# DMA transposes in the first DFT step of batches 2 to 7 and in half of batch 0's turn

## The chip, the cores and the metric

The kernel runs on one core of one Trainium2 chip. The number that counts is device time in microseconds (us), the median of several runs. Beside it stands one profiled execution, from which all durations below come. A core has TensorE (PE; its weight loads are listed as PEld), VectorE (DVE), ScalarE (ACT), GpSimd (POOL) and SyncE (SP); each works through its own instructions in order, and semaphores tie them together. DMAs are issued by SP (plain and transposing) and by POOL (those that cast from f32 to f16), and 16 DMA engines carry them out.

## The reference, cut to what matters

```python
def _attn_ref(x, w_r, w_i, b_r, b_i):            # x: 8 x 3008 x 256
    X = np.fft.rfft(x, axis=1)
    Xr, Xi = X.real, X.imag
    Yr = Xr @ w_r - Xi @ w_i + b_r
    Yi = Xr @ w_i + Xi @ w_r + b_i
    Yr = np.sign(Yr) * np.maximum(np.abs(Yr) - 0.01, 0.0)
    Yi = np.sign(Yi) * np.maximum(np.abs(Yi) - 0.01, 0.0)
    return np.fft.irfft(Yr + 1j * Yi, n=x.shape[1], axis=1)

def _moe_ref(x, w_in, w_out, s, b):              # x: 24064 x 256, d_ff 2048
    r = np.maximum(x @ w_in, 0.0)
    return (s * (r * r) + b) @ w_out
```

The output of the first function, seen as 24064 rows, is the input of the second. Inputs and output are float32.

## The kernel before, in words

The length 3008 is 94 x 32, so each transform is done in two DFT steps, both as matmuls with f16 tables: one over n1 (94 points, giving 96 rows that the code calls kappa), one over n2 (32 points). Kappa rows come in groups of four, so a pair table works on 128 rows (4 kappa x 32 n2), 24 pairs in all (NPAIR; H is 12).

For one batch the steps are:

- **s1** (`s1_units`): first DFT step over n1. 16 units; each multiplies x16 (f16 copy of x, 94 rows) by A_t, which is the stationary operand, with 512 columns of x moving. The result u (96 rows) goes to DRAM (ud, four stores of 384 KB) and comes back (us, four loads of 384 KB) with (kappa, n2) on the partitions.
- **s23** (`s23_units`): second forward step with F_t, channel mixing with W_t and W_g, soft threshold, rows put together in `ring` by small SP DMAs, first inverse step with T_t, result v. v goes to DRAM (vd, six stores) and comes back as vs (two loads of 768 KB) with kappa on the partitions.
- **s4** (`s4_units`): last inverse step with C_t, result yt, transposed for the feed-forward part.

Then come the tiles of the feed-forward part: `first_mm` (w_in, then Relu on ACT and square on DVE or ACT) and `second_mms` (w_out, then scale and bias on DVE, then the store). A tile has 16 values of mc; one value is a slot. The dictionary `plan` says which units of s1, s23 and s4 of later batches are put into which slot, and `schedule(start, span, units)` spreads them evenly. `mark[b]` is the slot of batch b's first tile; a period from one mark to the next has 96 slots, or 80 for batch 2. While the tiles of batch b-2 run, s1 of batch b and s23 of batch b-1 run in the same period, and s4 of batch b-1 ends just before mark[b-1]. `evac` moves a PSUM result to SBUF on ACT or DVE, whichever has less in the running sum `load`. Pools limit what may be alive at once: us has five buffers of a quarter batch, vs two halves, u three chunks, the output buffers ost three.

Batch 0 (`first_batch`) is handled alone, since nothing runs beside it yet. Its own first step writes ut with channels on the partitions, the mixing is done before the second forward step (`mix`, `fwd_dft`, `inv_dft`, 12 steps of i), and the result vt (channel half ec on partitions) is turned by TensorE with an identity: `turn(ec, k)`, eight matmuls and an evacuation of 1024 columns into vs, for k in 0 to 3 and both ec. `last_dft` then does the last step. While this goes on, the compact tables F_c and T_c are loaded and copied into zeroed block tables: `place_f(0)` and `place_f(1)` on ACT, `place_f_2` and `place_t` on DVE. A few units of batch 1's s1 run at the end (`some`), six are left for the first slots of the main loop (`schedule(0, 10, more)`). POOL loads x of batch 1, w_in and w_out after a gate on T_c, then makes W_g, the bounds, and w_sum (a sum over w_out); `make_bias` in slot 15 multiplies w_sum by ones on TensorE (L336).

The order within each engine is not exactly that of the source: the tile layer that records the program places the instructions. Each DMA also waits for the DMA eight places earlier on its queue, whose semaphore it takes over.

Of the kernel before, what the change touches and what calls it, by code (L numbers as in the profile page):

```python
# [9 lines left out]
F16 = mybir.dt.float16  # L10
F32 = mybir.dt.float32
# [3 lines left out]
P = 128  # L15
# [81 lines left out]
def kernel(  # L97
# [26 lines left out]
    F_d = nc.inline_tensor(fwd.astype(np.float16), name="dft_fwd").ap()  # L124
    T_d = nc.inline_tensor(inv.astype(np.float16), name="dft_inv").ap()
# [14 lines left out]
    upool = ctx.enter_context(tc.tile_pool(name="up", bufs=3))  # L140
    uspool = ctx.enter_context(tc.tile_pool(name="usp", bufs=5))
# [3 lines left out]
    vspool = ctx.enter_context(tc.tile_pool(name="vsp", bufs=2))  # L145
# [70 lines left out]
    b_g = cpool.tile([P, 2, D], F32, name="b_g")  # L216
# [4 lines left out]
    F_c = uspool.tile([P, NPAIR, 2, N2], F16, name="F_c", tag="us")  # L221
    b_h = cpool.tile([P, D], F16, name="b_h")
# [4 lines left out]
    sel_t = cpool.tile([P, P], F16, name="sel_t")  # L227
    T_c = uspool.tile([P, NPAIR, 64], F16, name="T_c", tag="us")
# [9 lines left out]

    def emit_load_forward():
        nc.sync.dma_start(  # L240
            out=F_c[:, 0:H].rearrange("p q r k -> p q (r k)"), in_=F_d[:, 0:H]
        )
        nc.sync.dma_start(out=sel_t, in_=S_d)

    def emit_load_inverse():
        nc.sync.dma_start(
            out=F_c[:, H:].rearrange("p q r k -> p q (r k)"), in_=F_d[:, H:]
        )
        t_load = nc.sync.dma_start(out=T_c, in_=T_d)
        with tc.issue_after(t_load.ins):  # L250
            nc.sync.dma_start(out=eye_t, in_=E_d)
            nc.sync.dma_start(out=C_t, in_=C_d)
            for i, bv in enumerate((b_r, b_i)):
                nc.sync.dma_start(out=b_st[:, i], in_=bv.unsqueeze(0).to_broadcast([P, D]))
            nc.sync.dma_start(out=s_bc, in_=moe_s.unsqueeze(0).to_broadcast([P, 1]))
            nc.sync.dma_start(out=bb_bc, in_=moe_b.unsqueeze(0).to_broadcast([P, 1]))
# [15 lines left out]
    F_t = cpool.tile([P, NPAIR, P], F16, name="F_t")  # L272
    nc.vector.memset(F_t, 0.0)
    T_t = cpool.tile([P, NPAIR, P], F16, name="T_t")
    nc.vector.memset(T_t, 0.0)
    F_2 = [uspool.tile([P, H, P], F16, name="F_2", tag="us") for _ in range(2)]
    for f in F_2:
        nc.gpsimd.memset(f, 0.0)
# [21 lines left out]
    def place_f(h):  # L300
        q = slice(h * H, h * H + H)
        for a in range(2):
            r = slice(64 * a, 64 * a + 64)
            nc.scalar.copy(out=blocks(F_t)[r, q, :, a], in_=F_c[r, q])

    def place_f_2(h):

        q = slice(h * H, h * H + H)
        for a in range(2):
            r = slice(64 * a, 64 * a + 64)  # L310
            nc.vector.tensor_scalar_mul(
                out=blocks(F_2[h])[r, :, 0, a], in0=F_c[r, q, 1], scalar1=-1.0
            )
            nc.vector.tensor_copy(out=blocks(F_2[h])[r, :, 1, a], in_=F_c[r, q, 0])

    def place_t(h):
        q = slice(h * H, h * H + H)
        for i in range(4):
            r = slice(32 * i, 32 * i + 32)
            c = 64 * (i % 2)  # L320
            nc.vector.tensor_copy(out=T_t[r, q, c : c + 64], in_=T_c[r, q])
# [12 lines left out]
    def make_bias():  # L334
        ps = other_bank()
        nc.tensor.matmul(ps[:, 0:D], ones, w_sum, start=True, stop=True)  # L336
        for j in range(2):
            nc.scalar.activation(
                out=bias_bc[:, j], in_=ps[:, 0:D], func=AF.Copy, scale=bb_bc
            )  # L340

# [8 lines left out]
    def first_batch():  # L350
# [3 lines left out]
        for g in range(N2 // 4):  # L354
# [26 lines left out]
            if c == 2:  # L381
                with tc.issue_after(last_dve.ins):
                    nc.vector.memset(F_c[0:1, H, 0, 0:1], 0.0)
                    nc.vector.memset(T_c[0:1, 0, 0:1], 0.0)
                emit_load_inverse()
# [3 lines left out]
        with tc.issue_after(last_dve.ins), tc.issue_after(last_act.ins):  # L389
            place_f(0)  # L390
            place_f_2(0)

        gate = nc.gpsimd.tensor_copy(out=w_in_t[0][0:1, 0:1], in_=T_c[0:1, 0, 0:1])
# [6 lines left out]
        vt = bigpool.tile([P, DC, N2, 96], F16, name="vt", tag="corr")  # L400
        gs = {}
        zt = {}
        g_last = [None]

        def mix(ec, u):
# [10 lines left out]
            if u % 3 == 1:  # L416
                g_last[0] = nc.scalar.copy(out=g, in_=ps)
                load["act"] += 1.02
            else:
                g_last[0] = nc.vector.tensor_tensor(  # L420
                    out=g, in0=ps,
                    in1=b_g[:, :, ec * P : (ec + 1) * P].unsqueeze(1).to_broadcast([P, 4, 2, P]),
                    op=ALU.add,
                )
                load["dve"] += 1.2
# [29 lines left out]
        def inv_dft(ec, u):  # L455
            ps = other_bank()
            z = zt.pop((ec, u))
            for j in range(4):
# [5 lines left out]
                vt[:, ec, :, 16 * u : 16 * u + 16],  # L464
# [3 lines left out]
        for h in range(2):  # L468
            vs[(0, h)] = vspool.tile([96, HW, D], F16, name="vs", tag="vs")

        def turn(ec, k):
            ps = two_banks()
            for j in range(8):
                nc.tensor.matmul(
                    ps[0:96, j // 4, (j % 4) * P : (j % 4) * P + P],
                    vt[:, ec, 8 * k + j, :], eye_t, start=True, stop=True,
                )
            h, n = divmod(8 * k, HW)
            evac(
                vs[(0, h)][:, n : n + 8, ec * P : (ec + 1) * P],  # L480
                ps[0:96].rearrange("p h (j e) -> p (h j) e", e=P), 1024,
            )
# [3 lines left out]
        def last_dft(ec, n2):  # L486

            ps = [one_bank(), other_bank()]
            for j in range(8):
                h, k = divmod(n2 + j, HW)  # L490
                nc.tensor.matmul(
                    ps[j // 4][:, (j % 4) * 96 : (j % 4) * 96 + 96],
                    vs[(0, h)][:, k, ec * P : (ec + 1) * P], C_t,
# [8 lines left out]
        more = s1_units(1, True)  # L502
# [7 lines left out]
        for i in range(2 * U + 2):  # L510
# [6 lines left out]
            k = i - U - 2  # L517
            if 0 <= k < 4:
                turn(0, k)
            if 0 <= k - 1 < 4:  # L520
                last_dft(0, 8 * (k - 1))
            if i >= 2 * U:
                some(3)
            if i == 0:
                with tc.issue_after(g_last[0].ins):
                    place_t(0)
            if i == 1:
                with tc.issue_after(g_last[0].ins):
                    place_f(1)
            if i == 2:  # L530
                with tc.issue_after(g_last[0].ins):
                    place_f_2(1)
            if i == 3:
                with tc.issue_after(g_last[0].ins):
                    place_t(1)
            if i == 9:

                gate = nc.gpsimd.tensor_copy(out=low[0:1, 0, 0:1], in_=vt[0:1, 1, 0, 0:1])
# [4 lines left out]
        for k in range(4):  # L543
            turn(1, k)
            some(1)
            if k:
                last_dft(1, 8 * (k - 1))
        last_dft(1, 24)
# [3 lines left out]
    def s1_units(b, more_banks=False):  # L552

        ud = dpool.tile([96, N2, D], F16, name="ud", tag="ud")
        hold = {}

        def unit(i):
            c, j = divmod(2 * i, XCH)
            if j == 0:
                hold["u"] = upool.tile([P, XCH, D], F16, name="u", tag="u")  # L560
            ps = other_bank() if more_banks and i % 2 else one_bank()
# [4 lines left out]
            u = hold["u"]  # L566
            evac(u[0:96, j : j + 2, :], ps[0:96, :].rearrange("p (j d) -> p j d", j=2), 512)
            if j == XCH - 2:
                nc.sync.dma_start(
                    out=ud[:, c * XCH : (c + 1) * XCH, :], in_=u[0:96]  # L570
                )
            if i == N2 // 2 - 1:
                uv = ud.rearrange("k n d -> (k n) d").rearrange("(q p) d -> p q d", p=P)
                for q in range(4):
                    t = uspool.tile([P, 6, D], F16, name="us", tag="us")
                    nc.sync.dma_start(out=t, in_=uv[:, 6 * q : 6 * q + 6, :])
                    us[(b, q)] = t

        return [lambda i=i: unit(i) for i in range(N2 // 2)]

    def s23_units(b):
# [8 lines left out]
        def fwd_unit(i):  # L590
# [3 lines left out]
            t = us[(b, i // 3)]  # L594
            for j in range(2):
                q = (2 * i + j) % 6
                for dc in range(DC):
                    nc.tensor.matmul(  # L598
                        ps[:, :, dc, j, :], t[:, q, dc * P : (dc + 1) * P],
# [53 lines left out]
        def inv_unit(i):  # L653
# [15 lines left out]
            if i == H - 1:  # L669
                vv = vd.rearrange("q (k n) e -> (q k) (n e)", n=N2)  # L670
                for h in range(2):
                    t = vspool.tile([96, HW, D], F16, name="vs", tag="vs")
                    nc.sync.dma_start(
                        out=t.rearrange("k n e -> k (n e)"),
                        in_=vv[:, h * HW * D : (h + 1) * HW * D],
                    )
                    vs[(b, h)] = t
# [17 lines left out]
    def s4_units(b):  # L695
# [6 lines left out]
        def unit(g):  # L702
# [5 lines left out]
            for j in range(w):  # L708
                h, k = divmod(n2 + j, HW)
                nc.tensor.matmul(  # L710
                    ps[:, j * 96 : (j + 1) * 96],
                    vs[(b, h)][:, k, ec * P : (ec + 1) * P], C_t,
# [148 lines left out]
    def load_x_2():  # L861
        emit_load_x(2, us[(1, 3)][0:1, 0, 0:1])
# [5 lines left out]
    schedule(0, 10, more)  # L868
# [4 lines left out]
    for b in range(2, B):  # L873
        s0, s1, s2 = mark[b - 2], mark[b - 1], mark[b]
        p = s1 - s0
        schedule(s0 + 40, p - 48, s1_units(b))
# [48 lines left out]
```

## Time and profile before

| what | us |
|---|---|
| median of 3 runs (851.32 to 852.76) | 851.42 |
| profiled execution | 851.2 |
| its span, first to last instruction | 849.4 |
| first L761 (feed-forward) matmul | 49.6 |
| first Relu (L768) | 52.1 |
| w_out landed / w_sum ready / its matmul L336 | 39.5 / 49.0 / 56.4 |
| tiles of batch 3's period begin | 342.0, 359.2, 376.6, 394.7, 412.3, 427.7 |

The page counts, per engine, the time in which an instruction ran. A matmul is pipelined, so its duration is longer than its share of TensorE; the distance between two starts shows the share. A line of the form "out<-in xcount | busy, mean | idle before, releaser" names a group by source line, engine and shapes. L160 and L164 are the two lines of `evac` and stand for many evacuations, told apart by the tile they write.

### The profile page before, as it was taken

How to read it: one execution, taken by the hardware profiler on the slowest of the kernel's cores; microseconds unless marked ns; L12 is line 12 of the kernel's file. 1: busy time of each engine (PE TensorE's matmuls, PEld its weight loads, DVE VectorE, ACT ScalarE, POOL GpSimd, SP SyncE). 2: the span in 40 equal slices, each digit the busy share in tenths (PEclk: the TensorE clock that was granted, in tenths of full speed). 3: DMA queues.
4: the chain of work that ended last, by engine and by line, in shares of the span. 5: the costliest groups of instructions: out<-in, count | busy, mean ns of one | idle time of the engine just before them, and what ended most of it. 6: DMA issues, size and time to landing. Idle time of an engine off the chain costs nothing.

```text
span 849.4 us, 17085 instructions
## 1 busy us (share of the span) xinstructions
PE 835.0 (98%) x6645; PEld 600.5 (71%) x6645; DVE 697.0 (82%) x1027; ACT 643.2 (76%) x856; POOL 46.6 (5%) x72
## 2 busy tenths in 40 slices
PE   8899999999999999999999999999999999999997
PEld 7757777777677766777677776777667777766765
DVE  6898987888888987888878888888977888776674
ACT  5898887787778787787777887787877787766673
POOL 5321000000000000000000000000000000000000
PEclk9999999999999999999999999999999999999999
DMA  7937457324761367324662247613354223411111
GB/s 165 161 104 162 108 148 185 101 76 100 177 186 54 92 159 184 109 78 103 171 177 65 74 106 199 172 40 92 100 156 118 62 79 98 112 33 38 38 44 50
DMA packets 105458, 95.07 MB, mean 112 GB/s; under 512 B 9510, under 2 KB 97578, under 8 KB 104034
## 3 DMA queue, kind: packets, MB, share of 16 engines
q1 hardware_dynamic: 98930, 79.57, 32.6%
q0 software_dynamic: 6448, 14.42, 10.7%
q8 instruction: 52, 0.85, 0.4%
q14 instruction: 28, 0.23, 0.1%
HBM read 52.54 MB, written 46.66 MB: 117 GB/s over the span
## 4 chain that ended last, share of the span: by engine, by line
PE 88%; DVE 4%; ACT 3%; DMA 2%; issue 1%; POOL 0%; SPq 0%; DVEq 0%; ACTq 0%; POOLq 0%
PE psa L832 36%; PE psh L761 36%; PE psf L627 4%; PE psf L562 2%; PE psf L613 2%; PE psf L598 2%; PE psf L657 2%; PE psf L710 2%; ACT rt L768 1%; DVE gt L775 1%; DMA x<-in_x_dram 1%; DMA out_dram<-ost 1%; PE psh L410 1%; ACT yt L160 0%; ACT vs L160 0%
## 5 line engine op out<-in xcount | busy, mean ns | idle before, releaser
L768 ACT ACTIVATE rt<-psh 128x1024 f32<-128x1024 f32 (+2 forms) x384 | 387.1, 1009 | 119.1 <-PE psh L761 117.7
L775 DVE TENSOR_TENSOR gt<-rt 128x1024 f16<-128x1024 f32 (+2 forms) x321 | 384.0, 1199 | 98.1 <-ACT rt L768 97.4
L832 PE MATMUL psa<-w_out_t,gt 128*128 128x256 f16 (+1 forms) x3024 | 454.3, 272 | 0.1
L832 PEld LDWEIGHTS <-gt 128*128 128x128 f16 (+1 forms) x3024 | 300.9, 101 | 187.2 <-issue 1.7
L761 PE MATMUL psh<-yt,w_in 128*128 128x512 f16 (+1 forms) x1344 | 396.7, 378 | 0.3 <-ACT rt L768 0.3
L761 PEld LDWEIGHTS <-w_in 128*128 128x128 f16 x1536 | 142.9, 98 | 27.4 <-issue 2.1
L842 DVE SCALAR_TENSOR_TENSOR ost<-psa,s_bc,bias_bc 128x512 f32<-128x512 f32 (+2 forms) x97 | 71.0, 732 | 8.3 <-PE psa L832 7.1
L772 ACT ACTIVATE gt<-rt 128x1024 f16<-128x1024 f32 (+2 forms) x63 | 66.2, 1050 | 1.0
L632 DVE TENSOR_TENSOR ring<-psf,s 128x512 f16<-128x512 f32 x84 | 57.5, 684 | 3.7 <-PE psf L627 2.9
L160 ACT CAST v<-psf 128x512 f16<-128x512 f32 x78 | 45.3, 582 | 18.7 <-PE psf L657 18.7
L160 ACT CAST xf<-psf 128x512 f16<-128x512 f32 x82 | 47.9, 585 | 10.9 <-PE psf L598 10.8
L160 ACT CAST u<-psf 96x512 f16<-96x512 f32 x77 | 44.5, 580 | 11.0 <-PE psf L562 10.7
L761 PE MATMUL psh<-tail,w_in 128*128 128x512 f16 (+1 forms) x192 | 52.1, 353 | 0.0
L627 PE MATMUL psf<-W_g,xf 128*128 128x256 f16 x336 | 50.4, 273 | 0.0
L160 ACT CAST yt<-psf 128x480 f16<-128x480 f32 (+2 forms) x75 | 38.1, 520 | 13.6 <-PE psf L710 13.6
L189 POOL DMA_DIRECT2D x<-in_x_dram x36 | 18.9, 530 | 429.3 <-PE psf L562 428.0
L562 PE MATMUL psf<-x,A_t 94*96 94x512 f16 x104 | 39.7, 381 | 1.7 <-ACT yt L160 0.5
L638 DVE TENSOR_TENSOR ring<-ring,high 128x512 f16<-128x512 f16 x84 | 35.5, 423 | 2.3
L639 DVE TENSOR_TENSOR ring<-ring 128x512 f16<-128x512 f16 x84 | 35.5, 422 | 1.9
L637 DVE TENSOR_TENSOR ring<-ring,low 128x512 f16<-128x512 f16 x84 | 35.4, 421 | 1.6
L627 PEld LDWEIGHTS <-xf 128*128 128x128 f16 x336 | 32.9, 98 | 3.8
L710 PE MATMUL psf<-C_t,vs 96*128 96x96 f16 x448 | 33.0, 205 | 0.1
(89 smaller groups left out, 501.9 us busy)
## 6 DMA issues: line engine op xcount, KB each, us to landing
out_dram<-ost SPq DMA_DIRECT2D x152, 128.0 KB
ud<-u SPq DMA_DIRECT2D x28, 384.0 KB
us<-ud SPq DMA_DIRECT2D x28, 384.0 KB
vd<-v SPq DMA_DIRECT2D x42, 256.0 KB
vs<-vd SPq DMA_DIRECT2D x14, 768.0 KB
x<-in_x_dram POOLq DMA_DIRECT2D x28, 376.0 KB, 5.9
ring<-ring SPq DMA_DIRECT2D x280, 32.0 KB
out_dram<-ost SPq DMA_DIRECT2D x16, 120.0 KB
```

The source lines that it names most:

```text
L160: return None, nc.scalar.copy(out=dst, in_=src)
L562: nc.tensor.matmul(ps[0:96, :], A_t[0:N1, :], x16[(b, c)][0:N1, j * D : (j + 2) * D], start=True, stop=True,)
L627: nc.tensor.matmul(ps[:, r, :], xt[:, 2 - r, dc], W_g[:, dc, r], start=(dc == 0), stop=(dc == DC - 1),)
L632: nc.vector.tensor_tensor(out=t, in0=ps, in1=hold[i // 2][:, i % 2].unsqueeze(1).to_broadcast([P, 2, D]), op=ALU.add,)
L638: nc.vector.tensor_tensor(out=m, in0=m, in1=high, op=ALU.min)
L710: nc.tensor.matmul(ps[:, j * 96 : (j + 1) * 96], vs[(b, h)][:, k, ec * P : (ec + 1) * P], C_t, start=True, stop=True,)
L761: nc.tensor.matmul(o, w_in_t[dc][:, mc * P : (mc + 1) * P], r, start=(dc == 0), stop=(dc == DC - 1),)
L768: nc.scalar.activation(out=rt[:, :, 0:w], in_=ps[:, :, 0:w], func=AF.Relu)
L772: nc.scalar.activation(out=gt[:, :, 0:w], in_=rt[:, :, 0:w], func=AF.Square)
L775: nc.vector.tensor_tensor(out=gt[:, :, 0:w], in0=rt[:, :, 0:w], in1=rt[:, :, 0:w], op=ALU.mult)
L832: nc.tensor.matmul(ps[0:size, h, :], gts[(ti, mc // 2)][:, mc % 2, sub * size : (sub + 1) * size], w_out_t[:, mc, :], start=(mc == 0), sto ...
L842: nc.vector.scalar_tensor_tensor(out=ost[0:size, 0:k], in0=ps[0:size, 0:k], scalar=s_bc[0:size], in1=bias_bc[0:size, 0:k], op0=ALU.mult, o ...
```

## The change

Three things are changed.

1. For batches 2 to 7 (`late=True`) s1 takes x16 as the stationary operand and A_t (96 columns) as the moving one: 16 units of four matmuls, giving u with channels on the partitions. At the last unit two transposing DMAs on SP, one per half of the channels (128 x 3072 elements of f16 each), write us directly; ud and its stores and loads are gone for these batches. us is now one tile per batch. s1 ends at 28 slots before the mark; it begins 28 slots after the period's start (40 for batch 2). Batch 1 keeps the old way.
2. The second half of F_t and of F_2, and all of T_t, are loaded as whole block tables, zeros included; `place_t`, `place_f(1)` and `place_f_2(1)` are gone.
3. In batch 0 the half ec = 0 of vt (padded from 96 to 128 kappa columns, the padding zeroed by POOL) is turned by one transposing DMA of 128 x 4096 elements instead of four calls of `turn`; it is issued at i = 7. All 16 units of batch 1's s1 run inside `first_batch`: two per step from i = 8 on, and the rest in the closing loop. `last_dft` for both halves comes in the closing loop.

Pools: us, u and vs have one (larger) buffer each; b_g, b_h and sel_t move into the pool of the tails.

```diff
     def emit_load_inverse():
-        nc.sync.dma_start(
-            out=F_c[:, H:].rearrange("p q r k -> p q (r k)"), in_=F_d[:, H:]
-        )
-        t_load = nc.sync.dma_start(out=T_c, in_=T_d)
+        nc.sync.dma_start(out=T_t[:, 0:H], in_=t_d[:, 0:H])
+        nc.sync.dma_start(out=F_t[:, H:], in_=f_d)
+        nc.sync.dma_start(out=F_2[1], in_=f_2_d)
+        t_load = nc.sync.dma_start(out=T_t[:, H:], in_=t_d[:, H:])
...
-        gate = nc.gpsimd.tensor_copy(out=w_in_t[0][0:1, 0:1], in_=T_c[0:1, 0, 0:1])
+        gate = nc.gpsimd.tensor_copy(out=w_in_t[0][0:1, 0:1], in_=F_t[0:1, H, 0:1])
...
+        def turn_by_dma(ec):
+            nc.sync.dma_start(
+                out=vs[0][:, :, ec * P : (ec + 1) * P],
+                in_=vt[ec].rearrange("p n k -> p (n k)"),
+                transpose=True,
+            )
...
-            k = i - U - 2
-            if 0 <= k < 4:
-                turn(0, k)
-            if 0 <= k - 1 < 4:
-                last_dft(0, 8 * (k - 1))
-            if i >= 2 * U:
-                some(3)
-            if i == 0:
-                with tc.issue_after(g_last[0].ins):
-                    place_t(0)
...
+            if i == U + 1:
+                turn_by_dma(0)
+            if i >= U + 2:
+                some(2)
...
-        for k in range(4):
-            turn(1, k)
-            some(1)
-            if k:
-                last_dft(1, 8 * (k - 1))
-        last_dft(1, 24)
+        for k in range(5):
+            if k < 4:
+                turn(1, k)
+            if k:
+                for ec in range(DC):
+                    last_dft(ec, 8 * (k - 1))
+            some(1)
...
+        def unit_late(i):
+            g, dc = divmod(i, DC)
+            if i == 0:
+                hold["u"] = upool.tile([P, DC, 96, N2], F16, name="u", tag="u")
+            u = hold["u"]
+            c, h = divmod(g, 2)
+            ps = one_bank()
+            for j in range(4):
+                lo = (4 * h + j) * D + dc * P
+                nc.tensor.matmul(
+                    ps[:, j * 96 : j * 96 + 96], x16[(b, c)][0:N1, lo : lo + P],
+                    A_t[0:N1, :], start=True, stop=True,
+                )
+            evac(
+                u[:, dc, :, 4 * g : 4 * g + 4],
+                ps[:, 0:384].rearrange("p (n k) -> p k n", k=96), 384,
+            )
+            if i == N2 // 2 - 1:
+                us[b] = uspool.tile([P, NPAIR, D], F16, name="us", tag="us")
+                for dc in range(DC):
+                    nc.sync.dma_start(
+                        out=us[b][:, :, dc * P : (dc + 1) * P],
+                        in_=u[:, dc].rearrange("p k n -> p (k n)"),
+                        transpose=True,
+                    )
...
-    schedule(0, 10, more)
+    assert not more
...
-        schedule(s0 + 40, p - 48, s1_units(b))
+        lead = 40 if b == 2 else 28
+        schedule(s0 + lead, p - lead - 28, s1_units(b))
```

In the program of the changed kernel SP's order at the end of s1 is: first transpose, a vd store, out stores, second transpose, the last vd store, then the two vs loads. The matmul that reads w_sum stands on TensorE after 8 feed-forward matmuls of the first tile, where it stood after 20.

## The prediction

> **What bounds the kernel now.** I read the page's busy line and groups first, then busy time by stretch, then the timeline where the change acts.
>
> ```profile
> PE 835.0 (98%) x6645; PEld 600.5 (71%) x6645; DVE 697.0 (82%) x1027; ACT 643.2 (76%) x856; POOL 46.6 (5%) x72
> L562 PE MATMUL psf<-x,A_t 94*96 94x512 f16 x104 | 39.7, 381 | 1.7 <-ACT yt L160 0.5
> L710 PE MATMUL psf<-C_t,vs 96*128 96x96 f16 x448 | 33.0, 205 | 0.1
> ```
> The page: TensorE never rests for long, and neither of these groups waits. Their mean durations (381 and 205 ns) overlap, so cost is the distance from one start to the next.
>
> ```profile
> 415.33 0.38 PE L562 MATMUL psf<-x,A_t 94*96 94x512 f16 x1
> 415.55 0.59 PE L761 MATMUL psh<-yt,w_in 128*128 128x512 f16 x2
> 429.45 0.59 PE L710 MATMUL psf<-C_t,vs 96*128 96x96 f16 x10
> 429.88 0.60 PE L761 MATMUL psh<-tail,w_in 128*128 128x512 f16 x2
> 412.01 0.36 SPq L666 DMA_DIRECT2D vd<-v  x1
> 415.59 0.37 SPq L666 DMA_DIRECT2D vd<-v  x1
> 418.34 0.80 SPq L673 DMA_DIRECT2D vs<-vd  x2
> ```
> Timelines of TensorE and of SyncE, batch 3: a 512-column matmul moves TensorE on by 0.22 us, a 96-column one with its own weights by 0.43/10 = 0.043 us. The last vd store leaves at 415.59, the vs loads at 418.34, and their reader L710 starts at 429.45.
>
> ```profile
> 17.00:20.00 3.00, 2.86 (x34) 2.56 (x34) 2.83 (x7) 2.92 (x5) 2.76 (x6) 1.00 0.45 63
> 30.00:35.00 5.00, 4.58 (x64) 3.99 (x62) 3.47 (x4) 4.12 (x8) 2.06 (x3) 1.00 1.23 199
> 49.60:60.50 10.90, 10.49 (x64) 5.12 (x62) 9.76 (x12) 10.68 (x17) 0.00 (x0) 1.00 0.28 85
> 97.00:116.50 19.50, 19.50 (x146) 14.79 (x144) 18.09 (x38) 16.89 (x25) 1.04 (x2) 1.00 0.60 134
> 288.50:307.40 18.90, 18.83 (x140) 13.24 (x138) 17.80 (x36) 16.11 (x23) 0.52 (x1) 1.00 0.37 88
> 394.70:412.30 17.60, 17.60 (x127) 12.17 (x125) 15.99 (x30) 14.44 (x21) 1.03 (x2) 1.00 0.59 126
> 418.30:427.00 8.70, 8.70 (x60) 5.71 (x58) 6.14 (x7) 6.15 (x8) 0.52 (x1) 1.00 0.89 225
> 440.30:447.50 7.20, 7.20 (x60) 5.01 (x58) 5.91 (x6) 4.75 (x7) 1.22 (x1) 1.00 0.85 234
> ```
> Busy time by stretch (PE, PEld, DVE, ACT, POOL, clock, DMA share, GB/s). From 60 us on TensorE bounds, with DVE and ACT at 75 to 94%. Before, up to 60 us, ACT and DVE bound: in 49.6 to 60.5 ACT is busy 10.68 of 10.90. The DMA engines are full around 30 to 35 and are filled again by the vs loads (418.3) and the us loads (440.3).
>
> **Part 1: first DFT step of batches 2 to 7.** Removed per batch: 16 L562 matmuls of 512 columns, 16 x 0.22 = 3.5 us. Added: 64 of 96 columns, the shape of L710 (96 x 128 weights, 96 columns), 64 x 0.043 = 2.75 us. Saved 0.77, six times: **-4.6 us**, straight off TensorE. The evacuations (384 columns in place of 512) cost 0.48 on ACT and 0.56 on DVE in the ut rows of batch 0, against 0.58 and 0.68, so they bring no new bound.
>
> The units move from slots 40 to 88 of a period into 28 to 68 (batch 2: 40 to 68; batch 4, whose period has 80 slots: 28 to 52). Two places get crowded: in 97.0 to 116.5 (batch 2) 9.1 units of 0.5 us replace 5.3 of 0.6, +1.4 us of vector work beside 34.98 of 39.0; in 288.5 to 307.4 (batch 4) +0.5 beside 33.91 of 37.8. Nothing if all fits, the whole plus queueing (2.5) if nothing does: I take **+1.0**.
>
> **Part 2: DRAM round trip replaced by two DMA transposes.** Gone are 4 ud stores and 4 us loads per batch (24 of each). Added are two transposes of 128 x 3072 halves, 786 KB each, on SP's queue. The trace has none. By bytes, at the 225 GB/s of the vs loads, the pair takes 7.0 us. By pieces: the us loads move 3072 rows of 512 bytes in 7.2 us, the pair moves 6144 rows of 256 bytes, 14.4 us at that pace. I take 9, nearer the bytes, because the page's queue line moves rows of all sizes at 79.57 MB in 32.6% of the span, 287 GB/s, whatever is mixed.
>
> What is queued behind: the last vd store, then vs<-vd, then out stores, all on SP. The penultimate unit falls in slot 63, some 411.2 by tile edges, plus 1.1 for its evacuation: T1 leaves at 412.3. Then pair + 2.75 (vd store to vs issue, 415.59 to 418.34) + 4.35 (half of the 8.7 us of the vs loads) must be over by 429.45: the pair may take **10.1 us**. At 9 it is hidden and costs 0; at 7 too; at 14.4 it costs 4.3 us of standing TensorE in each of six periods, 26 us. The fwd DFT needs us only some 34 us after T1, which hides even the slow end. The out stores have three ost buffers at one pair per 8.7 us, so a queue held by less than some 17 us stops nothing there.
>
> One skill rule agrees with the cheap end, one speaks hard against the change. The Trainium skill, "DMA: Bandwidth & Descriptors", Latency and other measured facts, gives 261 GB/s for a DMA transpose; as an estimate that is 6.0 us a pair and no stall. The Trainium skill, "VectorE: DVE Perf Modes", The three transpose paths, gives 1309 ns for a 128 x 128 block by DMA against 390 on TensorE and sends such blocks to TensorE; as an estimate, 24 blocks are 31 us, the pair 63, a stall of 53 per period and a total near 1,170. No row here shows either.
>
> **Part 3: the start.** From 14.6 to 52.1 us (first relu) I count 70.5 us of ACT and DVE work in 75. Removed: place_t, 1.52 + 1.44; second place_f_2, 1.20; second place_f, 1.66; four of eight turn evacuations (six at 1.01, two at 1.21), 4.25: 10.1 us. Added: four evacuations of batch 1's first step that ran after 52.1, 4 x 0.63 = 2.5. Net -7.6 over two engines that are 94% full: **-4.0**. The first tile loses those four: 2.5/2 = **-1.25**. TensorE's share (32 turn matmuls out, 4 L562 in) hides behind them.
>
> What comes late in its place. Table loads grow from 576 to 1536 KB: 960 KB at 225 GB/s are 4.3 us, about half of which fits where the DMA share was 0.45. Batch 0's transpose (1 MB, 4.7 us by bytes, 9.4 by pieces) leaves near 29.5 us, while w_in and w_out fill the engines. So w_out, landed at 39.5 before, lands at 41.5 to 48, and POOL's chain to w_sum (39.6 to 49.0) ends 9.4 us later, 51 to 57.5. The matmul that reads w_sum (L336) came after 20 L761 matmuls at 56.4, with 7.4 us to spare; in the new order it stands after 8, near 48. There TensorE's whole queue stands, and ACT and DVE after they have drained two pairs (2 us): 1 to 7.5. The transpose itself is wanted near 41, before the first last-DFT matmul: in time, or up to 2 late, which overlaps the other wait. I take **+3.5** (bounds 0 and 7.5).
>
> **Sum.** -4.6 + 1.0 + 0 - 4.0 - 1.25 + 3.5 = -5.35. The profiled execution took 851.2 us (span 849.4 and 1.8 around it), the median of the three runs is 851.42, so both bases agree: **846 us**. Its own range, 841.5 to 849.5.
>
> **Rivals.**
> - Nothing is late (pair fast, w_out lands before 42): 851.2 - 4.6 - 5.25 + 0.5 = 841.9 and a little under. For: in the stretch 40 to 45 us the DMA share is 0.00 now, so there is room to catch up. Against: the engines full at 30 to 35. Chance 0.16.
> - Pile-up at the start: 7.5 in place of 3.5, 850; POOL's sum becomes the bound, and the change all but vanishes. For: the reordered L336. Against: ACT and DVE drain while it waits. Chance 0.12.
> - Slower: the pair holds vs<-vd, and L710 stands. For: same queue, vs loads already 8.7 us long, and only 1.1 us to spare. It costs 6 us for each us of the pair beyond 10.1; the forecast's 5.35 are gone at 11.0, and at 14.4 the time is 872. Against: over the whole stretch 427.7 to 445.1 the DMA share is 0.61, so what is late can still be caught up within the step. Chance 0.26.
>
> **How the numbers follow.** Forecast 0.46, and the rivals as above. 0.2%, 1.7 us, is about what a measurement of this kernel can tell from no change. Faster: 0.46 + 0.16 + 0.04 of the pile-up; same 0.08 of it; slower 0.26. The lower end, 839, leaves out part of the best case; the upper, 862, holds pairs up to 12.7 us; together less than 0.2 is outside. The sign cases lie apart, hence 841.5 to 849.5 beside it.
>
> **What would show it.** Right: matmuls of the new first step 0.043 apart; the vs loads issued by 424 in batch 3's terms; L710 without idle time; first relu near 48 to 51. Wrong: TensorE waiting for vs or for w_sum by more than the terms above, transposes whose packets last beyond 10 us a pair, or DVE and ACT without a gap in slots 28 to 68. If the main loop per period does not shorten by 0.7 us, part 1 is mis-sized.

## The result, and the profile after

| what | before | after |
|---|---|---|
| median, us (4 runs each, side by side) | 852.09 | 896.97 |
| range | 851.32 to 853.16 | 892.39 to 901.12 |
| span of the profiled execution | 849.4 | 896.7 |
| first feed-forward matmul, tile 1 begins | 49.6, 60.5 | 54.4, 64.4 |
| from the first feed-forward matmul to the end | 799.8 | 842.3 |

The changed kernel is slower: ratio 1.0525, 95% interval 1.0468 to 1.0581. Of the 47.3 us between the two spans 4.8 lie before the first feed-forward matmul and 42.5 behind it.

The page of the changed kernel: busy line, shares of the chain that ended last, and the group that is L710 in the kernel before and L736 now (busy, mean ns | idle before it, and what ended that).

```profile
PE 843.3 (94%) x6901; PEld 609.9 (68%) x6901; DVE 685.4 (76%) x1005; ACT 637.8 (71%) x861; POOL 47.6 (5%) x72
...
PE 77%; DMA 10%; DVE 7%; issue 2%; ACT 2%; POOL 1%; SPq 1%; DVEq 0%; POOLq 0%
...
L736 PE MATMUL psf<-C_t,vs 96*128 96x96 f16 x448 | 37.1, 220 | 31.7 <-DMA vs<-vd 31.4
```

The group that waited 0.1 us now waits 31.7, for vs. Its waits, by the list of TensorE's waits (total, times, longest):

```profile
PE psf L736 <- DMA vs<-vd: 31.4, 6, 8.1
PE psf L506 <- DMA vs<-vt: 6.6, 1, 6.6
```

Six waits for vs, one in each period with transposes, and one in the start for batch 0's transpose. One of the six in full, batch 3's period: the timeline of SyncE's queue (start, duration of the issue), then of TensorE.

```profile
442.27 3.70 SPq L579 DMA_TRANSPOSE us<-u  x1
446.08 0.50 SPq L694 DMA_DIRECT2D vd<-v  x1
446.70 1.42 SPq L820 DMA_DIRECT2D out_dram<-ost  x2
448.58 5.78 SPq L579 DMA_TRANSPOSE us<-u  x1
454.48 0.51 SPq L694 DMA_DIRECT2D vd<-v  x1
...
457.08 0.81 SPq L701 DMA_DIRECT2D vs<-vd  x2
```
```profile
456.07 0.59 PE L787 MATMUL psh<-yt,w_in 128*128 128x512 f16 x2
456.50 0.60 PE L858 MATMUL psa<-w_out_t,gt 128*128 128x256 f16 x4
...
458.24 0.60 PE L858 MATMUL psa<-w_out_t,gt 128*128 128x256 f16 x4
462.84 0.98 PE L736 MATMUL psf<-C_t,vs 96*128 96x96 f16 x10 [4.01 <-DMA vs<-vd]
463.62 1.05 PE L787 MATMUL psh<-tail,w_in 128*128 128x512 f16 x2
464.47 1.06 PE L858 MATMUL psa<-w_out_t,gt 128*128 128x256 f16 x4
```

Two things are to be seen. SP needs 3.70 us to hand over the first transpose and 5.78 for the second, where each plain DMA beside them takes 0.3 to 0.8, and the vs loads leave 14.8 us after the first transpose. And the cost doesn't end with the wait: the two 512-column matmuls at 463.62 move TensorE on by 0.85 us, at 456.07 (full clock) by 0.43. TensorE ran at half its clock from 461.2 for 6.83 us. Windows of the same place (busy us of PE, PEld, DVE, ACT, POOL; granted clock; DMA share; GB/s):

```profile
447.00:457.00 10.00, 10.00 (x72) 6.86 (x71) 7.68 (x7) 5.72 (x7) 0.00 (x0) 1.00 1.11 207
457.00:463.00 6.00, 1.99 (x16) 1.18 (x15) 2.13 (x3) 2.69 (x3) 0.00 (x0) 0.85 0.90 229
```

Counted from the moment at which the next matmul could have begun, the six waits last 8.2, 6.4, 5.2, 4.2, 6.4 and 2.1 us, 32.4 in all (the list above counts from the end of the matmul before and has 31.4). Half-clock stretches (3.41 to 10.24 us, 41.0 in all) start in or just behind each; what of them lies after TensorE resumed costs half its length, 12.8 us. Together 45.2.

The start: the transpose on SP's queue, w_sum on POOL, and TensorE.

```profile
29.42 16.45 SPq L494 DMA_TRANSPOSE vs<-vt  x1
...
46.37 1.15 POOL L331 TENSOR_TENSOR acc<-w_out_t 128x512 f32<-128x512 f16 x1 [10.13 <-DMA w_out_t<-in_moe_w_out_dram]
...
48.23 0.50 PE L506 MATMUL psf<-C_t,vs 96*128 96x96 f16 x4 [6.57 <-DMA vs<-vt]
...
57.40 0.27 PE L340 MATMUL psa<-w_sum,ones 128*128 128x256 f16 x1
```

SP is held for 16.45 us by one transpose while the w_in and w_out loads fill the DMA engines; w_out lands at 46.3 instead of 39.5, TensorE stands for 6.6 us before the first last-DFT matmul, and its clock is half from 44.8 to 51.6.

### The profile page after: what moved, and what is told of

Same layout as the page of the kernel before. It is cut to its first block, busy times and chain, and to the rows that moved or that the text cites. A ratio compares the mean times of both kernels' runs of the same rounds, so it can differ in the third digit from the quotient of the medians.

```text
span 896.7 us, 17520 instructions
## 1 busy us (share of the span) xinstructions
PE 843.3 (94%) x6901; PEld 609.9 (68%) x6901; DVE 685.4 (76%) x1005; ACT 637.8 (71%) x861; POOL 47.6 (5%) x72
## 3 DMA queue, kind: packets, MB, share of 16 engines
q1 hardware_dynamic: 119090, 72.16, 32.4%
## 4 chain that ended last, share of the span: by engine, by line
PE 77%; DMA 10%; DVE 7%; issue 2%; ACT 2%; POOL 1%; SPq 1%; DVEq 0%; POOLq 0%
PE psa L858 32%; PE psh L787 32%; DMA vs<-vd 4%; PE psf L655 3%; DVE gt L801 3%; PE psf L736 3%; DMA vs<-vt 2%; PE psf L641 2%; PE psf L626 2%; PE psf L568 2%; PE psf L685 1%; DMA vd<-v 1%; DVE ring L660 1%; ACT rt L794 1%; DMA x<-in_x_dram 1%
## 5 line engine op out<-in xcount | busy, mean ns | idle before, releaser
L787 PEld LDWEIGHTS <-w_in 128*128 128x128 f16 x1536 | 138.5, 99 | 14.7 <-issue 1.2
L868 DVE SCALAR_TENSOR_TENSOR ost<-psa,s_bc,bias_bc 128x512 f32<-128x512 f32 (+2 forms) x97 | 71.0, 732 | 11.5 <-PE psa L858 11.4
L736 PE MATMUL psf<-C_t,vs 96*128 96x96 f16 x448 | 37.1, 220 | 31.7 <-DMA vs<-vd 31.4
L171 ACT CAST yt<-psf 128x480 f16<-128x480 f32 (+2 forms) x72 | 35.7, 517 | 42.8 <-PE psf L736 42.5
L175 DVE CAST yt<-psf 128x480 f16<-128x480 f32 (+2 forms) x34 | 21.2, 624 | 55.4 <-PE psf L736 48.6
L660 DVE TENSOR_TENSOR ring<-psf,s 128x512 f16<-128x512 f32 x84 | 57.5, 684 | 3.7 <-PE psf L655 3.4
L171 ACT CAST u<-psf 128x384 f16<-128x384 f32 (+1 forms) x94 | 46.1, 491 | 17.2 <-PE psf L568 9.0
L736 PEld LDWEIGHTS <-vs 96*128 96x128 f16 x448 | 31.4, 106 | 36.4 <-DMA vs<-vd 33.1
L787 PE MATMUL psh<-tail,w_in 128*128 128x512 f16 (+1 forms) x192 | 54.6, 367 | 0.0
```

The costliest lines, as they stand in the source:

```text
L171: return None, nc.scalar.copy(out=dst, in_=src)
L660: nc.vector.tensor_tensor(out=t, in0=ps, in1=hold[i // 2][:, i % 2].unsqueeze(1).to_broadcast([P, 2, D]), op=ALU.add,)
L736: nc.tensor.matmul(ps[:, j * 96 : (j + 1) * 96], vs[b][0:96, n2 + j, ec * P : (ec + 1) * P], C_t, start=True, stop=True,)
L787: nc.tensor.matmul(o, w_in_t[dc][:, mc * P : (mc + 1) * P], r, start=(dc == 0), stop=(dc == DC - 1),)
L868: nc.vector.scalar_tensor_tensor(out=ost[0:size, 0:k], in0=ps[0:size, 0:k], scalar=s_bc[0:size], in1=bias_bc[0:size, 0:k], op0=ALU.mult, o ...
```

## The experiments

"Half clock" is always a stretch of granted clock 0.5. Each run's kernel before ran on the same chip (medians 851.3 to 851.9).

**1. The transposes behind the vs loads.** The sixteen units stay where they are; the two transposes move out of the last unit into an entry of the plan one slot later, to be issued after the vs loads of the batch before.

```diff
-            if i == N2 // 2 - 1:
-                us[b] = uspool.tile([P, NPAIR, D], F16, name="us", tag="us")
+        def transposes():
+            us[b] = uspool.tile([P, NPAIR, D], F16, name="us", tag="us")
+            with tc.issue_after(vs_load[b - 1].ins):
...
+        plan.setdefault(s1 - 27, []).append(transposes)
```


> The two transposes of each batch are held on SP's queue until the vs loads of the batch before them have been issued; nothing else changes. Theory A (in the changed kernel the vs loads stand behind both transposes on SP's queue, so the last DFT step stands still for 33.0 us in six places, and after each the TensorE clock is granted at half for 3.4 to 10.2 us, another 17 us): all of that goes, 897 - 50 = 847 us (844 to 851), no idle time before L736's matmuls, the half clock only at both ends of the run and after the start's own wait. Rival B (the transposes cost DMA time wherever they stand, and the wait only moves to the first matmuls that read us): 880 us or more, with TensorE idle before the forward DFT. Rival C (the denser slots of the new first step are what costs): above 870 without such idle time.

Measured: 855.36 us, ratio 1.0049 (1.0032 to 1.0066), 4.4 above the range expected. Timeline of SP and the same group of this run:

```profile
426.71 0.80 SPq L704 DMA_DIRECT2D vs<-vd  x2
427.62 11.87 SPq L582 DMA_TRANSPOSE us<-u  x2
```
```profile
L739 PE MATMUL psf<-C_t,vs 96*128 96x96 f16 x448 | 33.2, 205 | 0.6
```

The six waits are gone, and with them all half clock between the first tile and the end. From the first feed-forward matmul to the end it takes 798.4 us; the difference to the changed kernel, 43.9, agrees with the 45.2 counted above. The transposes still hold SP for 12 us, but nothing urgent stands behind them. This is the cause of nearly the whole loss; what is left over the kernel before lies in the start (first feed-forward matmul at 55.2).

**2. Batch 0's turn by TensorE again**, the transposes of batches 2 to 7 as in the change.

```diff
-                    vt[ec][:, 8 * k + j, :], eye_t, start=True, stop=True,
+                    vt[ec][:, 8 * k + j, 0:96], eye_t, start=True, stop=True,
...
-            if i == U + 1:
-                turn_by_dma(0)
+            if 0 <= i - U - 2 < 4:
+                turn(0, i - U - 2)
```


> Only batch 0's transpose is undone: its first half is turned by four calls of turn again, at the steps where the kernel before had them; the steady part stays as changed. Theory A (the start is late because the transpose took from 29.4 to 48.2 us and TensorE waited 6.9 us for it, then ran 6.8 us at half clock, 3.4 more): minus 6.9, minus 3.4, plus 2.3 for four evacuations, 897 - 8 = 889 us (887 to 891); first feed-forward matmul near 47, w_out landed near 41 in place of 46.3. Rival (the larger table loads crowd the DMA engines whoever turns): w_out still lands at 45 or later, and the time falls by 2 us or less.

Measured: 898.94 us (1.0554, 1.0536 to 1.0572), a miss. The list of TensorE's waits of this run:

```profile
PE psf L736 <- DMA vs<-vd: 39.6, 6, 11.2
PE psa L340 <- POOL w_sum L336: 2.8, 1, 2.8
```

The first feed-forward matmul did come 6.0 us earlier, at 48.3, but tile 1 only 2.1 earlier, at 62.2: w_out landed at 44.0, so the larger table loads alone delay it by 4.5 us, and TensorE now stands for w_sum. What that saved was lost in the six waits, which were longer in the profiled execution (39.6 for 31.4); why they were is not shown. The total alone would mislead here.

**3. Dummy matmuls in front of the wait.** 80 matmuls of 128 columns whose result nobody reads, ahead of the first last-step matmul of batches 1 to 6.

```diff
+            if g == 0 and b < B - 1:
+                ps = one_bank()
+                for _ in range(80):
+                    nc.tensor.matmul(ps[:, 0:P], ones, ones, start=True, stop=True)
```


> The changed kernel with 80 matmuls of 128 columns on ones, 4.4 us at full clock, before the first matmul of the last DFT step of batches 1 to 6; they add work and feed nothing. The waits stay. Theory A (half clock follows from TensorE having stood still): the waits shrink to at most 4 us of idle time, most half-clock stretches of the main loop go, 17 us less and some 2 us of overshoot: 882 us (878 to 888). Rival (the clock is lowered by something else that happens there, the transposes or the crowded DMA engines): the stretches stay and the time is 897 to 903.

Measured: 899.29 us (1.0552, 1.0525 to 1.0579), a miss in time. The half-clock stretches of the main loop fell from six (41.0 us) to two (13.7 us), as expected of the theory that the clock follows the standing. But dummies (26.8) and remaining gaps (14.9) together made 41.7 us where the changed kernel stood 32.4, and that took back the 8.8 us that the clock gave (its cost behind the waits fell from 12.8 to 4.0); the second transpose of the third period took SP 11.4 us instead of 4.0. The clock's part is shown by the profile, not by the time.

**4. Experiments 1 and 2 together.**

```diff
+            with tc.issue_after(vs_load[b - 1].ins):
...
+                turn(0, i - U - 2)
```


> The transposes behind the vs loads and batch 0 turned by TensorE, so that of the change the new first step and the whole tables remain. Theory A: both gains add, 897 - 50 - 8 = 839 us (835 to 846), faster than the kernel before. Rival B or C: above 860.

Measured: 852.20 us (1.0003, 0.9988 to 1.0019): the waits are gone, yet the 839 expected for the rest of the change didn't come. Tile 1 begins at 62.8 (before: 60.5), and from there to the end it takes 788.3 (before: 788.9). The new first step's gain is missing. Over tiles 6 to 38, five batches, the distances between starts of TensorE's matmuls add up to:

```text
                                        before   this run
the first step's own matmuls             17.56     13.70
the 130 matmuls ring,T_t                 14.81     17.49
all others                              518.27    519.07
sum                                     550.64    550.26
```

The gain of 3.86 us is there, 0.77 per batch. 2.68 of it go again behind the matmuls that read the ring, 0.80 elsewhere. (The expectations below call 0.95 and 3.62 what the sums of the ring matmuls hold beyond 13.86.) Sorted by what follows them, 24 of these matmuls have a unit of the first step behind them, which starts 0.246 us later in the mean; behind all others the next matmul starts 0.11 later.

**5. The start as before.** Experiment 4 with compact tables, their copies on ACT and DVE, and six units of batch 1's first step left for slots 0 to 10.

```diff
-    assert not more
+    schedule(0, 10, more)
...
+            if i == 0:
+                with tc.issue_after(g_last[0].ins):
+                    place_t(0)
```


> Edit: the whole start of the kernel before (compact tables placed by ACT and DVE, all eight turns by TensorE, six units of batch 1's first step left for the slots 0 to 10 of the main loop), and the main loop of e4_both (new first step for batches 2 to 7, transposes behind the vs loads, the change's slots). Theory: in e4_both the start costs 2.3 us (tile 1 at 62.8 in place of 60.5) and the main loop gains 0.6; taking the larger tables back gives those 2.3, less the six units that go back into the main loop (6 x 0.22 = 1.3 us of TensorE, which e4_both had in its start). 850.5, between 849.5 and 851.5; w_out lands near 39.5 and its matmul waits for nothing; tile 1 near 60.5. Rival: the larger tables cost nothing in the end, and e4_both stands where it does because of the main loop: 852 to 853.5, tile 1 near 60.5 and the main loop longer than 790.

Measured: 851.87 us (0.9999, 0.9990 to 1.0007), above the range expected by 0.4 and just below the rival's. Tile 1 begins at 61.1 (62.8 in experiment 4), w_out lands at 40.6, and the matmul that reads w_sum waits for nothing. The larger tables and the reordered start thus cost about 1.8 us up to tile 1; the six units take 0.7 of that back behind it (789.0 from tile 1 to the end, 788.3 in experiment 4). The new first step still brings nothing.

**6. Gentler slots.** Experiment 5 with the first step later and more spread out.

```diff
-        lead = 40 if b == 2 else 28
+        lead = 40 if b == 2 else 36
...
-        schedule(s0 + lead, p - lead - 28, units)
-        plan.setdefault(s1 - 28 + 1, []).append(transposes)
+        schedule(s0 + lead, p - lead - 18, units)
+        plan.setdefault(s1 - 18 + 1, []).append(transposes)
```


> Edit: e5_start_as_before with the first step of batches 3 to 7 spread over slots 36 to 78 of a period in place of 28 to 68 (batch 2: 40 to 78; batch 4: 36 to 62), and the transposes issued 18 slots before the period's end, still behind the vs loads. Theory: the excess behind the matmuls that write the ring (3.62 us over five batches, 0.95 before) and behind the others comes from units packed more densely than ACT and DVE empty the PSUM banks; spread out it is mostly gone, some 2 to 2.5 us: 848, between 846.5 and 849.5, excess of the ring matmuls below 2. Rival 1: the density does not come from the packing (it belongs to four small matmuls with their own weights per unit): same time as e5_start_as_before within 0.7. Rival 2: the transposes end too late for the second forward step: TensorE idle before the matmuls that read us, in each period, and 852 or more.

Measured: 855.69 us (1.0043, 1.0021 to 1.0066), nearest to the second rival, though TensorE waits in two periods and not in each. From the list of TensorE's waits:

```profile
PE psf L629 <- DMA us<-u: 5.2, 3, 2.3
```

us comes too late in two periods; in batch 4's the two issues took SP 16.4 and 9.5 us. The ring matmuls fell only from 17.40 in experiment 5 to 16.49. With the later slots 11 of them instead of 23 are followed by a unit of the first step, at 0.319 us instead of 0.249; behind the others it is 0.11 as before. So the place of the loss is the shared slot, but spreading the units did not make it cheaper.

**7. Free slots.** Back to experiment 5's ending, but in batches 3, 5, 6 and 7 the units go where the plan has no other unit. That was prompted by this place in experiment 5's timeline of TensorE:

```profile
397.37 0.60 PE L863 MATMUL psa<-w_out_t,gt 128*128 128x256 f16 x4
397.80 0.38 PE L688 MATMUL psf<-ring,T_t 128*128 128x256 f16 x2
398.45 0.33 PE L569 MATMUL psf<-A_t,x 94*128 94x96 f16 x4 [0.27 <-DVE ring L663]
398.62 0.60 PE L792 MATMUL psh<-yt,w_in 128*128 128x512 f16 x2
```

Two 256-column matmuls move TensorE on by 0.22 us, but the next begins 0.65 later: a unit of the other step and one of the first step stand in the same slot, and the second waits for a bank of the two-bank pool psf. In the period of 96 slots the units of s23 leave every third slot free, and with 16 units over 48 slots from slot 40 the kernel before hits only free ones. Over 40 slots from 28 they fall on ten taken ones by the plan (the expectation says eight), five of them with matmuls that read the ring.

```diff
+            free = [i for i in range(s0 + 22, s1) if i not in plan][:16]
+            for i, u in zip(free, units):
+                plan.setdefault(i, []).append(u)
+            plan.setdefault(free[-1] + 1, []).append(transposes)
```


> Edit: e5_start_as_before, but for batches 3, 5, 6 and 7 the 16 units of the first step go into slots of the period that hold no other unit (22, 25, ... 64, 67) in place of every 2.5th slot from 28 to 65; the transposes leave one slot earlier, still behind the vs loads. Batches 2 and 4 as in e5_start_as_before. Theory: in the kernel before, three slots apart, the units of these batches fell into free slots by the arithmetic of the plan (only the period of 80 slots had shared ones); 2.5 slots apart, 8 of 16 share a slot with a unit of the other step, mostly the first inverse one, and the second of the two waits for a PSUM bank that is not yet empty. That is the excess of 3.5 us behind the ring matmuls. In free slots most of it goes: over tiles 6 to 38 548.0 us in place of 550.8, the pairs ring matmul, then first step below 1.2 us; time 849.3, between 848 and 850.3. Rival: the excess comes from ACT and DVE being fuller over the whole stretch, wherever the units stand: it moves to other neighbours of the first step, the sum over tiles 6 to 38 stays within 0.8 of 550.8 and the time within 0.8 of e5_start_as_before.

Measured: 848.59 us, ratio 0.9970 (0.9959 to 0.9981). Tiles 6 to 38 take 547.48 us (550.77 in experiment 5), the ring matmuls 14.85 of it (17.40); only four of them, in batch 4's period, are still followed by a unit of the first step. The page of experiment 5, and then of this run:

```profile
L569 PE MATMUL psf<-A_t,x 94*128 94x96 f16 x384 | 32.1, 205 | 2.6 <-DVE ring L663 1.0
```
```profile
PE 831.7 (98%) x6933; PEld 605.4 (71%) x6933; DVE 693.2 (82%) x1023; ACT 638.7 (75%) x860; POOL 46.5 (5%) x72
...
L569 PE MATMUL psf<-A_t,x 94*128 94x96 f16 x384 | 32.2, 206 | 0.6 <-ACT u L160 0.3
```

The same matmuls wait 0.6 us instead of 2.6. This version beats the kernel before by 0.3%, clear of the noise, and the changed kernel; batches 2 and 4 keep the shared slots.

**8. The transposes issued by ACT**, at the change's place in the program.

```diff
-                    nc.sync.dma_start(
+                    nc.scalar.dma_start(
                         out=us[b][:, :, dc * P : (dc + 1) * P],
```


> Edit: the changed kernel with the two transposes of each of batches 2 to 7 issued by ACT in place of SP; place in the program and start unchanged. Theory A (the vs loads are late because SP is held, by 3.7 us for each transpose and by the stores that it waits for between the two): the vs loads leave SP within 4 us of the last vd store, as in the kernel before, and the waits before the first last-step matmul fall from 32.4 us in six periods to below 10; ACT is held by the two issues in turn, 7 us or more per period, and the Relus behind them make TensorE wait for part of it. 870 to 890. Theory B (the transposes' packets fill the DMA engines, whoever issues them): the vs loads leave early, but their packets last until the transposes are done, the waits stay above 20 us and the time at 895 or more.

Measured: 912.47 us, one run. The list of TensorE's waits, and ACT's timeline in batch 3's period:

```profile
PE psh L787 <- ACT rt L794: 40.7, 7, 16.7
```
```profile
453.59 3.61 ACTq L579 DMA_TRANSPOSE us<-u  x1
...
458.29 9.45 ACTq L579 DMA_TRANSPOSE us<-u  x1
467.84 1.94 ACT L794 ACTIVATE rt<-psh 128x1024 f32<-128x1024 f32 x2 [8.65 <-issue]
```
SP's queue in the same place:
```profile
459.10 0.36 SPq L694 DMA_DIRECT2D vd<-v  x1
469.02 0.80 SPq L701 DMA_DIRECT2D vs<-vd  x2
```

Neither theory is right as stated. TensorE doesn't wait for vs at all, as A has it, but only because it stands for the Relus instead, which stand behind ACT's issue. And with nothing else in SP's way the vs loads still left 9.9 us after the last vd store (8.9 to 9.9 in four of six periods, 2.5 to 5.5 in the kernel before), as B has it: by the packet records that store's data ran only from 464 to 468, beside those of the second transpose. So the hold isn't a property of SP's queue: the engine that issues is held, and the store beside it is slow as well. Moving the issue elsewhere doesn't help; moving it behind the urgent loads does.

**9. The next x held back until vs has landed.** In the changed kernel the last unit of the first step also frees the last x buffer. POOL sends the load into it at 444.15 in batch 3's period, and by the trace's packets it runs from 447 to 451, between the transposes.

```diff
-            plan.setdefault(s1 + 6, []).append(lambda b=b: emit_load_x(b + 1))
+            plan.setdefault(s1 + 6, []).append(lambda b=b: emit_load_x(b + 1, vs[b - 1][0:1, N2 - 1, D - 1 : D]))
```


> Edit: the changed kernel with the load of the next batch's x (1.5 MB in SBUF, four casting loads on POOL) held back until vs has landed, by a copy of one element of vs; all else unchanged. In the changed kernel the last unit of the first step also frees the last x buffer, so that the last of these loads (issued at 444.15 in batch 3's period, packets from 447 to 450) stands in the DMA engines between the two transposes. Theory: this load and the stores it delays are what stretches the pair from some 10 us of packets to 14.7 us from the first transpose's issue to the issue of the vs loads (mean of six). Without it: below 12.5; the waits before the first last-step matmul fall by 2 to 3 us each, from 32.4 in all to about 16, the half-clock stretches in the main loop from six to four or fewer, the time from 897 to between 866 and 882. Rival: the pair is long by itself (SP's issue of 3.7 us for each transpose, the stores that SP waits for between the two, the second transpose's issue while the first still runs): from first issue to vs loads above 13.5, waits of 26 or more, 888 or more.

Measured: 882.35 us (1.0371, 1.0354 to 1.0389), 0.35 above the range expected. SP's timeline and the waits of this run:

```profile
429.69 3.68 SPq L579 DMA_TRANSPOSE us<-u  x1
...
435.86 4.75 SPq L579 DMA_TRANSPOSE us<-u  x1
440.71 0.53 SPq L694 DMA_DIRECT2D vd<-v  x1
...
443.22 0.81 SPq L701 DMA_DIRECT2D vs<-vd  x2
```
```profile
PE psf L736 <- DMA vs<-vd: 18.2, 6, 4.3
```

From the first transpose to the vs loads it is now 12.4 us in the mean of six (14.7 in the changed kernel), the waits fall from 31.4 to 18.2, the half-clock stretches of the main loop from six to four (17.1 us in all). Against the kernel before on the same chip the loss is 31.1 us, where it was 44.9: the x load was worth some 14 us, about a third of the loss, and the rest stays without it.

## Why the prediction was wrong, step by step

The forecast was 846, between 839 and 862; 896.97 is beyond the slow rival's 872 too.

- **The step that failed: "At 9 it is hidden and costs 0"** (part 2). The price of the pair as data was about right: by the packet records of the trace the first transpose takes 4.0 us and the second 5.3 in batch 3's period, 9.3 together, and the pair 9.1 to 10.5 in four other periods (15.1 in the first). The sum treated the pair as nothing but data. From the first transpose's issue to the issue of the vs loads it should have been 9 + 2.75 = 11.75; it was 14.7 in the mean of six (12.1 to 16.6). Between the two transposes stand SP's own issue (3.7 us), stores, and the x load that the earlier end of the first step sets free: experiment 9 shows 2.3 us of it to be that load. Next, from the issue of the vs loads to the first matmul that reads them it took 6.1 us in the mean, not 4.35: by the packet records the data of the first half was through after 4.6, and 1.5 more passed before the matmul began, a term that the sum didn't have. And from the first transpose to the time when L736 was wanted there were 15.55 us in the mean, not 17.15. Together 2.95 + 1.75 + 1.6, less the 1.05 that the forecast had to spare, gives 5.25 per period; 31.4 / 6 = 5.2 was measured.
- **The price of a wait was too small as well.** The slow rival ("the pair holds vs<-vd, and L710 stands") had the mechanism and the place, at 6 us per us; but it had no term for the clock. Half clock after each wait added 12.8 us to 32.4. Waits and clock together are the loss of the main loop.
- **Part 1** held in size: 0.77 per batch, matmuls 42.8 ns apart. "Nothing if all fits, the whole plus queueing (2.5) if nothing does: I take +1.0" was too small and looked at the wrong thing: it priced the evacuations' sum on ACT and DVE, while the cost, 3.5 us in five batches (experiment 4), came from which slots are shared. Experiments 4, 5 and 7 show it: with the same units in free slots all but 0.7 of it is gone.
- **Part 3**: the vector work's shift was real (in experiment 2, with the four turn evacuations back, the first feed-forward matmul comes 1.3 us earlier than before), but "94% full" was not: the 70.5 us counted are durations that partly overlap, and the profile's windows have 64.6 busy of 75, 86%. "In time, or up to 2 late" for batch 0's transpose was wrong: it left at 29.4, as taken, and was 6.6 late. Its data ran from 33.3 to 47.7, 14.3 us where 4.7 to 9.4 were taken; its 4096 packets had a median of 31 ns beside the weight loads, the others' 18. w_out at 46.3 lay within the 41.5 to 48 given, w_sum at 55.7 within 51 to 57.5. The wait for w_sum, the +3.5 of the sum, did not come, since the transpose had already put off the matmul that reads it to 57.4; without that transpose it was 2.8 (experiment 2). The start lost 3.9 us up to tile 1, where -1.75 was the sum: 2.1 to 2.3 of it go with the transpose (the changed kernel against experiment 2, experiment 1 against 4), 1.8 with the larger tables and the new order (experiment 4 against 5).
- **The two rules of the skill.** The trace disagrees with both. One transpose of 786 KB in 4.0 us of packets (batch 3's period) is 195 GB/s, where the Trainium skill, "DMA: Bandwidth & Descriptors", Latency and other measured facts, has 261; and 4.0 us over 24 blocks of 128 x 128 is 0.17 us a block, far below the 1309 ns of the Trainium skill, "VectorE: DVE Perf Modes", The three transpose paths. The second had the direction right, and the size wrong by more than a factor of seven.

## What to carry to other kernels

A DMA costs its queue more than its bytes: count the issue, the latency and every DMA that the same step sets free, and put a long transfer behind, not in front of, a load that TensorE is about to read; in experiment 1, where the first matmul that reads it came 21 to 25 us after the issue, this cost no wait; in experiment 6, at 20 to 25 us and with longer issues, it cost 5.2 us. Price a wait of TensorE with the clock that follows. When units move to other slots, look at which units share a slot and a PSUM pool before adding up engine time.

## What was not expected of the hardware

- Issuing one transpose of 128 x 3072 f16 held the issuing engine for 3.6 to 3.7 us at best, SP and ACT alike, and for longer when other transfers kept the DMA engines busy: 5.8 us in the place shown above, 8 of the 11.87 us of experiment 1 for the first of the two, right behind the vs loads, and 16.4 at worst in experiment 6. A plain store beside it took 0.5.
- TensorE's clock was 0.5 in pieces of 3.41 us (3.41, 6.83, 10.24) around the waits for vs. A wait of 1.88 us, counted from the end of the matmul before, set it off (676.25 to 678.13 in the changed kernel, half clock from 679.6); in experiment 9 waits of 1.86 and 2.98 us did not, but 2.74 and 3.09 did. What tells them apart is where the wait lies: within each run all changes of the clock are whole steps of 3.413 us apart, and behind tile 1, over all runs, every such step at full clock in which TensorE stood for 1.88 us or more was followed by half clock, and none in which it stood for 1.80 or less. The 1.88 us lie within one step; an edge of the steps cuts the 2.98 us into 1.49 and 1.49. Filling the wait with matmuls kept the clock up in four of six periods. The Trainium skill, "TensorE: Matmul & The Clock Gate", HAM oscillation, tells of a drop after a DMA wait that crosses an activity window; the steps of 3.41 us agree with the window of about 3.4 us that its Part 1 gives. The waits of 1.88 and 2.74 us show that less than such a length of waiting was enough here.
